# A completion semaphore of its own for the first value-weight load of a fused state-space and attention kernel

## The chip, the cores and the metric

The kernel runs on one core of one Trainium2 chip. The metric is the device time of one execution in microseconds (us). The profile gives the span from the first to the last instruction, which is about 1.8 us less than that time. Executions of one kernel within one group of runs differ by up to about 4 us (993.85 to 997.71 us in the widest case of the kernel before), and that scatter matters at the end of this text.

## The reference, cut to what matters

The reference mixes a diagonal complex state-space layer (A) and a 32-head softmax attention (B) over the same input x of 2048 rows and 1024 columns, with a gate for each row.

```python
x = A_x
g = _sigmoid((x * gate_w).sum(-1, keepdims=True))
a = _A_ref(x, A_Lambda_re, A_Lambda_im, A_B_re, A_B_im, A_C_re, A_C_im, A_log_dt, A_Dskip)
b = _B_ref(x, B_wqkv, B_wo)
return g * a + (1 - g) * b

# in _B_ref
scores = jnp.einsum("bhqd,bhkd->bhqk", q, k) * (Dh ** -0.5)
p = _softmax(scores, axis=-1)
o = jnp.einsum("bhqk,bhkd->bhqd", p, v)
```

The softmax takes 32 x 2048 x 2048 exponentials. The kernel does them on ScalarE in 1024 instructions of 128 partitions x 1024 columns.

## The kernel before

A recorder notes every operation in one order, with the tiles that it reads and writes, and works out the semaphore waits. Each DMA signals one of 14 completion semaphores, called lanes. DMAs take the lanes in turn, in the order in which they are recorded, whichever engine issues them. A DMA depends on the previous user of its lane, because the recorder counts completions by lane.

```python
# Sched.op
if dma:
    j = self.dma_rr
    self.dma_rr = (j + 1) % self.n_dma_lanes
    o.lane = "dma%d" % j
    prev = self.dma_lane_last[j]
    if prev is not None:
        d.append(prev)              # wait for the previous load on this lane
    self.dma_lane_last[j] = o
```

The order of recording at the start is this. Everything up to `opening()` is recorded before the first value-weight load, which is inside `opening()`.

```python
# build (begin() first: 2 weight loads, 9 pieces of x, 5 parameter rows: lanes in turn)
self.begin()
self.ld_b(0, 0)                    # two B tiles, real and imaginary, by SyncE
self.ld_b(1, 1)
for part in (1, 2, 0):
    self.ld_w(1, part)             # projection weights of the next head group
for j in range(8):
    self.ld_c(j)                   # 8 C tiles, real and imaginary: 16 transposes by SyncE
self.opening()
```

The opening works through a list of words. K stands for a key projection of 256 rows, B for a burst of scores with its two exponentials (a pair), Va and Vb for value projections, M for the parameters, P for a product of exponentials and values.

```python
OPENING = ("K0 B0 K1 M B1 K2 Va0 B2 Vb0 K3 Va1 B3 Vb1 Q1 Va2 K4 ..."   # cut
...
if op == "K":
    if i == 0:
        ...                        # first key and query projections
        evac(self.Q[:, 0, 0:256], 6, ("Q", 0), True, self.act)
        self.dma(lambda e: e.dma_start(self.wv0[:, :, 0:128], self.wsrc[:, :, 2048:2176]),
                 [], ["wv0"], "ld_w", "act")    # the load in question, in ScalarE's queue
```

Va0 is called "the first value product" below. The load stands in ScalarE's queue ahead of the first exponential. Va0, which reads it, stands in TensorE's queue ahead of the scores of burst B2. In the profile the load is the DMA into `f_OT` from `in_B_wqkv_dram`, as `wv0` lies in that tile.

## Time and profile before

| | before |
|---|---|
| time, median of 3 | 996.18 us (995.86 to 997.41) |
| ScalarE busy | 943.4 us (95%) |
| 1006 of the 1024 exponentials, the group written to `f_pt` | 922.8 us busy, 0.917 us each (busy time by count) |
| longest wait of ScalarE | 28.5 us, from 9.56 to 38.08 us |

The page's first rows show the stretch. Each digit is the busy share of one of 40 slices (24.9 us each) in tenths; PEclk is the granted TensorE clock in tenths.

```profile
PE   3399999999999999999999999999999999989996
ACT  0389999999999999999999999999999999999997
PEclk8599999999999999999999999999999999999998
DMA  9924203331113301321004401033201212223312
```

From the fourth slice on ScalarE is busy without a break. In the first two, TensorE is busy for about a third of the time and ScalarE for less, while the DMA engines are busy.

The exponentials are one group of the page (busy us, mean ns of one, idle time before them and what ended most of it). The mean of 1288 ns is longer than 0.917 us because the records of neighbours overlap; two in a row take 1.94 us.

```profile
L1527 ACT ACTIVATE f_pt<-f_ps 128x1024 bf16<-128x1024 f32 x1006 | 922.8, 1288 | 30.9 <-DMA f_cT_re<-in_A_C_re_dram 28.5
```

The chain of waits, as shares of the span by engine, and the waits of ScalarE (who waited for what: us in total, times, longest):

```profile
ACT 93%; SPq 3%; PE 2%; DMA 1%; DVE 1%; issue 0%; DVEq 0%
```

```profile
ACT f_pt L1527 <- DMA f_cT_re<-in_A_C_re_dram: 28.5, 1, 28.5
...
```

An exponential waits 28.5 us for a C tile, and it reads no C tile. The timeline (start in us, duration in us, engine, line, operation; idle time before it and its releaser in brackets) shows what lies between:

```profile
9.18 0.38 ACT L1125 ACTIVATE f_Q<-f_ps 128x256 bf16<-128x256 f32 x1 [3.29 <-PE f_ps L1100]
37.63 0.40 ACTq L1135 DMA_DIRECT2D f_OT<-in_B_wqkv_dram  x1
38.08 1.94 ACT L1527 ACTIVATE f_pt<-f_ps 128x1024 bf16<-128x1024 f32 x2 [28.51 <-DMA f_cT_re<-in_A_C_re_dram]
...
44.35 1.94 ACT L1527 ACTIVATE f_pt<-f_ps 128x1024 bf16<-128x1024 f32 x2 [2.41 <-PE f_ps L1521]
...
74.57 911.43 ACT L1527 ACTIVATE f_pt<-f_ps 128x1024 bf16<-128x1024 f32 x994
```

The wait belongs to the value-weight load, but its record is only 0.40 us long. The Trainium skill, "Perfetto Trace Analysis", section DMA Instruction — HWDGE (DVE, Sync), says that the profiler reports a DMA instruction from the moment when its semaphores are satisfied. This trace agrees: the record starts at 37.63 us and the wait shows only as idle time of the exponential behind it. So a DMA that blocks a queue is found by the idle time of its successor.

The last line of that timeline shows why the wait counts: 994 exponentials run from 74.57 us without a gap. Whatever ScalarE loses before, nothing makes up for.

The chain of waits in order of time (start in us, us, what) gives the rest of the story:

```profile
33.85 3.77 DMA f_cT_re<-in_A_C_re_dram
...
37.63 5.02 DMA f_OT<-in_B_wqkv_dram
...
42.70 1.05 PE f_ps L1148 x8
```

The C tile is issued at 33.85 us and lands 3.77 us later. Only then is the value-weight load issued, and it takes 5.02 us. TensorE's first value product (L1148) starts as soon as it has landed. Before the C tile, the chain is SyncE's queue from 0.91 us on, one transpose after the other, with three weight loads among them.

Last, the table by stretches of time (busy us and number of instructions of each engine, then the granted TensorE clock, the share of the DMA engines and GB/s):

```profile
14.00:38.00 24.00, 0.00 (x0) 0.00 (x0) 0.00 (x0) 0.00 (x0) 0.55 (x2) 0.53 1.15 203
```

From 14 to 38 us no matmul and no exponential runs, the clock falls to a mean of 0.53, and the DMA engines move 203 GB/s.

### The profile page before, as it was taken

How to read it: one execution, taken by the hardware profiler on the slowest of the kernel's cores; microseconds unless marked ns; L12 is line 12 of the kernel's file. 1: busy time of each engine (PE TensorE's matmuls, PEld its weight loads, DVE VectorE, ACT ScalarE, POOL GpSimd, SP SyncE). 2: the span in 40 equal slices, each digit the busy share in tenths (PEclk: the TensorE clock that was granted, in tenths of full speed). 3: DMA queues.
4: the chain of work that ended last, by engine and by line, in shares of the span. 5: the costliest groups of instructions: out<-in, count | busy, mean ns of one | idle time of the engine just before them, and what ended most of it. 6: DMA issues, size and time to landing. Idle time of an engine off the chain costs nothing.

```text
span 994.6 us, 33339 instructions
## 1 busy us (share of the span) xinstructions
PE 930.4 (94%) x15308; PEld 486.0 (49%) x15308; DVE 512.8 (52%) x1096; ACT 943.4 (95%) x1034; POOL 9.8 (1%) x39
## 2 busy tenths in 40 slices
PE   3399999999999999999999999999999999989996
PEld 1264464446444455444644554444554546444443
DVE  0178888788988823821238821158838111232223
ACT  0389999999999999999999999999999999999997
POOL 1000000000000000000000000000000000000000
PEclk8599999999999999999999999999999999999998
DMA  9924203331113301321004401033201212223312
GB/s 199 196 54 82 46 8 53 68 79 29 39 36 73 79 5 29 60 71 47 8 8 67 82 28 36 26 63 78 50 7 39 68 49 91 68 73 112 112 59 70
DMA packets 157074, 60.88 MB, mean 61 GB/s; under 512 B 145664, under 2 KB 145664, under 8 KB 156928
## 3 DMA queue, kind: packets, MB, share of 16 engines
q1 hardware_dynamic: 153728, 57.89, 26.0%
q8 instruction: 121, 1.98, 0.8%
q10 hardware_dynamic: 3200, 0.80, 0.4%
q14 instruction: 25, 0.20, 0.1%
HBM read 16.79 MB, written 12.58 MB: 30 GB/s over the span
## 4 chain that ended last, share of the span: by engine, by line
ACT 93%; SPq 3%; PE 2%; DMA 1%; DVE 1%; issue 0%; DVEq 0%
ACT f_pt L1527 92%; SPq L1032 2%; PE f_ps L1148 1%; ACT f_OT L1527 1%; SPq L1042 1%; PE f_ps L1111 1%; DMA f_OT<-in_B_wqkv_dram 1%; SPq L1048 0%; DMA f_cT_re<-in_A_C_re_dram 0%; SPq L1037 0%; DVE f_V L1153 0%; ACT f_Et L1527 0%; PE f_ps L1521 0%; DVE f_xT L1790 0%; DVE f_xT L1477 0%
## 5 line engine op out<-in xcount | busy, mean ns | idle before, releaser
L1527 ACT ACTIVATE f_pt<-f_ps 128x1024 bf16<-128x1024 f32 x1006 | 922.8, 1288 | 30.9 <-DMA f_cT_re<-in_A_C_re_dram 28.5
L1543 PEld LDWEIGHTS f_ps<-f_V,f_pt 128*128 128x128 bf16 x8048 | 234.2, 96 | 105.9 <-issue 105.6
L1543 PE MATMUL f_ps<-f_V,f_pt 128*128 128x33 bf16 x8048 | 285.4, 178 | 0.0
L1521 PE MATMUL f_ps<-f_Q,f_K 32*128 32x256 bf16 x4096 | 204.0, 274 | 52.3 <-ACT f_pt L1527 34.3
L1521 PEld LDWEIGHTS f_ps<-f_Q,f_K 32*128 32x128 bf16 x4096 | 60.6, 92 | 273.1 <-ACT f_pt L1527 240.5
L1409 PE MATMUL f_ps<-f_xT,f_wb 128*128 128x512 bf16 x512 | 131.0, 377 | 0.6
L1379 PE MATMUL f_ps<-f_xT,f_wb 128*128 128x512 bf16 x472 | 121.2, 378 | 0.1
L1328 DVE TENSOR_TENSOR_SCAN f_ht<-f_pf,f_init,f_ut 128x512 bf16<-128x512 f32 x64 | 81.0, 1275 | 0.0
L1453 DVE TENSOR_SCALAR f_Ag<-f_ps,f_gcol 128x512 f32<-128x512 f32 x32 | 24.0, 751 | 97.5 <-PE f_ps L1438 97.5
L1438 PE MATMUL f_ps<-f_cT_re,f_hp 128*128 128x512 bf16 x192 | 72.8, 379 | 0.3
L1438 PE MATMUL f_ps<-f_cT_im,f_hp 128*128 128x512 bf16 x192 | 72.6, 378 | 0.0
L1471 PE MATMUL f_ps<-f_wb,f_OT 128*128 128x512 bf16 x252 | 66.0, 381 | 0.0
L1556 DVE RECIPROCAL f_rc<-f_ps 128x8 f32<-128x8 f32 x63 | 13.1, 208 | 91.3 <-PE f_ps L1543 91.1
L1477 DVE SCALAR_TENSOR_TENSOR f_xT<-f_ps,f_gcol,f_hp 128x512 bf16<-128x512 f32 (+1 forms) x28 | 21.0, 751 | 75.3 <-PE f_ps L1471 75.3
L1397 PE MATMUL f_ps<-f_wb,f_xT 128*128 128x128 bf16 x896 | 59.2, 219 | 0.0
L1409 PEld LDWEIGHTS f_ps<-f_xT,f_wb 128*128 128x128 bf16 x512 | 40.5, 96 | 32.1 <-issue 0.7
L1415 DVE CAST f_ub<-f_ps 128x512 bf16<-128x512 f32 x48 | 33.2, 692 | 34.0 <-PE f_ps L1409 34.0
L1379 PEld LDWEIGHTS f_ps<-f_xT,f_wb 128*128 128x128 bf16 x472 | 36.8, 96 | 28.3
L1397 PEld LDWEIGHTS f_ps<-f_wb,f_xT 128*128 128x128 bf16 x896 | 50.4, 97 | 0.2
L1386 DVE CAST f_Q<-f_ps 128x512 bf16<-128x512 f32 x31 | 21.5, 692 | 49.2 <-PE f_ps L1379 49.0
L1319 DVE TENSOR_TENSOR f_tq<-f_ht,f_Et 128x512 bf16<-128x512 bf16 x128 | 46.1, 416 | 0.0
L1319 DVE TENSOR_TENSOR f_ut<-f_tq 128x512 f32<-128x512 bf16 x64 | 42.2, 684 | 0.0
(124 smaller groups left out, 493.0 us busy)
## 6 DMA issues: line engine op xcount, KB each, us to landing
ag_scratch<-f_Ag SPq DMA_DIRECT2D x32, 256.0 KB, 2.2
f_hp<-ag_scratch SPq DMA_DIRECT2D x32, 256.0 KB, 2.8
f_wb<-in_B_wqkv_dram SPq DMA_DIRECT2D x21, 256.0 KB, 4.2
out_dram<-f_xT SPq DMA_DIRECT2D x16, 256.0 KB, 2.1
f_wb<-in_B_wo_dram SPq DMA_DIRECT2D x1, 1024.0 KB, 6.5
f_OT<-f_On SPq DMA_TRANSPOSE x63, 2.3
f_wb<-in_B_wo_dram SPq DMA_DIRECT2D x1, 768.0 KB
f_wb<-in_B_wqkv_dram ACTq DMA_DIRECT2D x2, 256.0 KB, 4.3
```

The source lines that it names most:

```text
L1319: ops.append((c, lambda: dve(lambda e: e.tensor_tensor(o, a, b, op), r, w)))
L1328: ops.append((1.29, lambda ri=ri: dve(lambda e: e.tensor_tensor_scan(ht[:, ri, :], rr, ut[:, ri, :], self.init[:, ri, j:j + 1], ALU.mult, ...
L1379: mms.append((1, lambda e, f, l, a=a: e.matmul(ps[:, bank, :], w[:, g % 2, part, a, :], xT[:, a, 512 * ch:512 * (ch + 1)], start=f, stop=l ...
L1397: m = e.matmul(ps[:, bank, 128 * q:128 * (q + 1)], xT[:, a, 128 * kt:128 * (kt + 1)], w[:, g % 2, 2, a, :], start=(a == 0), stop=(a == 7))
L1409: mms.append((1, lambda e, f, l, a=a: e.matmul(ps[:, 7, :], bT[:, n % 2, ri, a, :], xT[:, a, 512 * ch:512 * (ch + 1)], start=f, stop=l), [ ...
L1415: self.dve(lambda e: e.tensor_copy(self.ub[k][:, ri, :], ps[:, 7, :]), [("bank", 7)], [("ub", k, ri)] + over, "evac_u")
L1438: mms.append((1, lambda e, f, l, j=j, ri=ri: e.matmul(ps[:, 7, :], hp[:, ri, j, cols], cT[ri][:, j, 512 * cb:512 * (cb + 1)], start=f, sto ...
L1453: self.dve(lambda e: e.tensor_scalar(a, ps[:, 7, :], self.gcol[:, 0, tt:tt + 1], None, ALU.mult), [("bank", 7), "g0"], [at], "evac_c")
L1471: mms.append((1, lambda e, f, l, j=j: e.matmul(ps[:, 7, :], OT[:, j, 256 * qb + 128 * r:256 * qb + 128 * (r + 1)], wo[j][0][:, 512 * cb:51 ...
L1521: m = e.matmul(ps[:, 2 * sl[h // 2] + h % 2, 256 * kl:256 * (kl + 1)], K[32 * h:32 * h + 32, g % 2, 128 * kt:128 * (kt + 1)], Q[32 * h:32 ...
L1527: self.act(lambda e, s=s, p=p: e.activation(self.tile[p], ps[:, 2 * s:2 * s + 2, :], ACT.Exp, scale=SCALE), [("S", s)], [("pt", p)], "exp")
L1543: m = e.matmul(ps[:, 6, o:o + 33], self.tile[p][:, h2, 256 * kl + 128 * qt:256 * kl + 128 * (qt + 1)], V[:, g % 2, 2 * i + kl, h, :], star ...
```

## The change

Its intent is to free the first value-weight load from the load that used its lane before. It adds a 15th semaphore that only this load uses; the other loads still take 14 in turn. Two signatures that pass the new argument on are cut.

```diff
-    def __init__(self, n_dma_lanes=12, pool_in_order=False, serial_xpose=False):
+    def __init__(self, n_dma_lanes=12, pool_in_order=False, serial_xpose=False, own=0):
+        self.n_rr = n_dma_lanes - own
...
         if dma:
-            j = self.dma_rr
-            self.dma_rr = (j + 1) % self.n_dma_lanes
+            j = lane
+            if j is None:
+                j = self.dma_rr
+                self.dma_rr = (j + 1) % self.n_rr
...
-  self.dma(lambda e: e.dma_start(self.wv0[:, :, 0:128], ...), [], ["wv0"], "ld_w", "act")
+  self.dma(lambda e: e.dma_start(self.wv0[:, :, 0:128], ...), [], ["wv0"], "ld_w", "act", 14)
...
-        S = Sched(n_dma_lanes=14)
+        S = Sched(n_dma_lanes=15, own=1)
```

The order of instructions is the same on every engine. The loads recorded after this one move down by one lane.

More of the change, by code (lines that the diff above doesn't have):

```diff
@@ L60, in lanes, with op @@
         return list(ENGINES) + ["dma%d" % i for i in range(self.n_dma_lanes)]
-    def op(self, eng, fn, reads=(), writes=(), deps=(), name="", dma=False, acc=(), xpose=False):
+    def op(self, eng, fn, reads=(), writes=(), deps=(), name="", dma=False, acc=(), xpose=False, lane=None):
         o = Op(eng, fn, name, dma)
@@ L1023, in pool, with dma @@
         return self.S.op("pool", fn, reads=r, writes=w, name=name)
-    def dma(self, fn, r, w, name="", eng="sp"):
-        return self.S.op(eng, fn, reads=r, writes=w, name=name, dma=True)
+    def dma(self, fn, r, w, name="", eng="sp", lane=None):
+        return self.S.op(eng, fn, reads=r, writes=w, name=name, dma=True, lane=lane)
     def ld_x(self, i, eng="sp"):
@@ L1134, in opening @@
                     evac(self.Q[:, 0, 0:256], 6, ("Q", 0), True, self.act)
-                    self.dma(lambda e: e.dma_start(self.wv0[:, :, 0:128], self.wsrc[:, :, 2048:2176]), [], ["wv0"], "ld_w", "act")
+                    self.dma(lambda e: e.dma_start(self.wv0[:, :, 0:128], self.wsrc[:, :, 2048:2176]), [], ["wv0"], "ld_w", "act", 14)
                 else:
```

## The prediction

> **What bounds the kernel now.** ScalarE's exponentials. The chain of waits gives 92% of the span to them, and the groups show 1006 of 128x1024 with 922.8 us busy, 0.917 us each; from 63.7 us to 983 us the chain is ScalarE without a break. TensorE is 94% busy but waits for ScalarE in that stage. So an idle stretch of ScalarE in the opening is paid in full. There is one: the waits of ScalarE show 28.5 us (9.56 to 38.08 us) ended by the DMA of a C tile.
>
> **Cause.** ScalarE issues the first value-weight load ("wv0") at 37.63 us, just before its first exponential. The instruction order with its waits shows that this load waits on a DMA lane. Loads take 14 lanes in turn in recording order; 39 loads (the B and C transposes too) are recorded first, so wv0 gets lane 11 behind the third C transpose, which SyncE issues at 33.85 us and which lands 3.77 us later. ScalarE's queue is in order, so the exponentials behind the load, whose scores were ready at 10.1 us, wait too. TensorE then idles until 38.9 us, and the windows show its clock fall to 0.50.
>
> **What the change does.** wv0 gets a 15th semaphore, never used before, and loses its wait. Loads recorded after wv0 move down one lane; the instruction order is equal on all engines.
>
> **Cost, step by step.**
> - wv0 issues at about 9.6 us (0.40 us of issue time), the first exponential starts near 10.1 us.
> - The DMA engines are busy from 0 to 54 us (about 200 GB/s, windows). wv0 took 5.02 us to land among C transposes; among x transposes I estimate 5 to 7: 14.6 to 16.6 us. The Trainium skill, "DMA: Bandwidth & Descriptors", section Queues, rings and completion order, says that each DMA engine takes turns between queue rows, so SyncE's backlog need not drain first; the 5.02 us, with that backlog, agree.
> - The first value product moves from 42.70 us to that landing; the third pair of exponentials from 44.35 to about 16.3 us: 28 us less.
> - x pieces must not bind: issue 7.1 to 20.0 us, landing 5.5 us later (median), so the last lands near 26 us plus 1.3 us for wv0's 256 KB; its K projection would run at about 30 us.
> - In the opening before, the matmuls of 39 to 46 us ran on the halved clock (K projection 1.89 and 1.60 us instead of 1.03). With an idle gap of 2 to 3 us only, most of that, about 0.5 to 1 us, is gained as well.
> - SyncE's queue is not moved and ends its C transposes at about 54 us; the first two output transposes (68 and 79 us before) then wait a little behind them, off the chain: their buffers and the next B tiles are needed 5 us or more later.
>
> All of it lies on the critical path, as ScalarE has no slack after.
>
> **Prediction: 967.5 us**, 8 in 10 between 965.5 and 971.5. Faster by over 2%: 0.96, within 2%: 0.03, slower: 0.01.
>
> **Signs.** ScalarE's 28.5 us wait gone, replaced by about 2 to 4 us before the third pair; wv0 issued at 9.6 us; exponentials unbroken from about 35 us; same 0.917 us each; granted clock near 1.0 in the opening; tail unchanged.
>
> **What would make it wrong.** wv0 landing late behind x transposes; x pieces landing later and stalling K projections; TensorE still cold; late output or B transposes stalling TensorE near 55 to 70 us.

## The result, and the profile after

| | before | after |
|---|---|---|
| time, median of 4 | 996.02 us (995.75 to 997.41) | 967.25 us (967.16 to 967.44) |
| ratio | 1 | 0.9709 (0.9692 to 0.9725) |
| span of the profiled execution | 994.6 us | 965.7 us |
| ScalarE busy | 943.4 us | 943.4 us |

A ratio here is the mean time of one kernel's runs over that of the other's in the same rounds, so it is not quite the ratio of the medians. The interval is a 95% interval. Executions over 1.5% slower than the fastest of the same kernel are left out of the means.

The page's first rows after the change:

```profile
PE   8999999999999999999999999999999999989995
ACT  4999999999999999999999999999999999999997
PEclk9999999999999999999999999999999999999998
```

The idle second slice is gone. ScalarE works the same 943.4 us in a span that is 28.9 us shorter. (TensorE's busy sum of 904.4 us is not comparable with 930.4 us before, as 223 matmul records are missing from this trace.)

The same group of exponentials, the chain's shares by engine, and the waits of ScalarE:

```profile
L1531 ACT ACTIVATE f_pt<-f_ps 128x1024 bf16<-128x1024 f32 x1006 | 922.8, 1288 | 2.4 <-PE f_ps L1525 2.4
```

```profile
ACT 95%; PE 3%; DVE 1%; DMA 1%; issue 0%; DVEq 0%
```

```profile
ACT L1069 <- issue: 4.5, 1, 4.5
ACT f_OT L1531 <- PE f_ps L1525: 4.4, 3, 2.5
ACT f_Q L1129 <- PE f_ps L1104: 2.9, 1, 2.9
ACT f_pt L1531 <- PE f_ps L1525: 2.4, 2, 1.8
```

SyncE's queue has left the chain, and the 28.5 us are gone. A wait of 1.8 us remains before the third pair. The timeline of ScalarE (its lines are numbered 4 higher than before):

```profile
8.83 0.38 ACT L1129 ACTIVATE f_Q<-f_ps 128x256 bf16<-128x256 f32 x1 [2.87 <-PE f_ps L1104]
8.83 0.40 ACTq L1139 DMA_DIRECT2D f_OT<-in_B_wqkv_dram  x1
9.80 1.94 ACT L1531 ACTIVATE f_pt<-f_ps 128x1024 bf16<-128x1024 f32 x2 [0.59 <-PE f_ps L1525]
...
15.49 1.94 ACT L1531 ACTIVATE f_pt<-f_ps 128x1024 bf16<-128x1024 f32 x2 [1.82 <-PE f_ps L1525]
...
45.73 911.41 ACT L1531 ACTIVATE f_pt<-f_ps 128x1024 bf16<-128x1024 f32 x994
```

The load is issued at 8.83 instead of 37.63 us, and the first exponential starts at 9.80 instead of 38.08 us. In the chain the load takes 5.00 us and is followed by the value product:

```profile
8.83 5.00 DMA f_OT<-in_B_wqkv_dram
13.84 0.05 issue
13.88 1.01 PE f_ps L1152 x8
```

The gain is made by then and is carried to the end unchanged. It is worked out here from the two traces:

| event | before | after | difference |
|---|---|---|---|
| first value product | 42.70 | 13.88 | 28.82 |
| third pair of exponentials | 44.35 | 15.49 | 28.86 |
| the 994 exponentials in a row | 74.57 | 45.73 | 28.84 |
| end of the span | 994.6 | 965.7 | 28.9 |

One thing did not come as forecast. In the table by stretches the clock of the profiled execution was again low for a while:

```profile
14.00:18.00 4.00, 4.00 (x38) 3.02 (x37) 1.37 (x7) 1.94 (x2) 0.21 (x1) 0.58 1.23 198
```

### The profile page after: what moved, and what is told of

It reads as the page before. It is cut to its first block, busy times and chain, and to the rows that moved or that the text cites. A ratio compares the mean times of both kernels' runs of the same rounds, so it can differ in the third digit from the quotient of the medians.

```text
span 965.7 us, 33117 instructions
## 1 busy us (share of the span) xinstructions
PE 904.4 (94%) x15085; PEld 486.2 (50%) x15308; DVE 512.9 (53%) x1096; ACT 943.4 (98%) x1034; POOL 9.8 (1%) x39
## 3 DMA queue, kind: packets, MB, share of 16 engines
q8 instruction: 121, 1.98, 0.9%
## 4 chain that ended last, share of the span: by engine, by line
ACT 95%; PE 3%; DVE 1%; DMA 1%; issue 0%; DVEq 0%
ACT f_pt L1531 95%; PE f_ps L1152 1%; ACT f_OT L1531 1%; PE f_ps L1086 1%; PE f_ps L1115 1%; DMA f_OT<-in_B_wqkv_dram 1%; PE f_ps L1104 0%; DVE f_V L1157 0%; ACT f_Et L1531 0%; PE f_ps L1525 0%; DVE f_xT L1794 0%; DVE f_xT L1481 0%; DVE f_ut L1749 0%; PE f_ps L1547 0%; ACT f_OT L1772 0%
## 5 line engine op out<-in xcount | busy, mean ns | idle before, releaser
L1531 ACT ACTIVATE f_pt<-f_ps 128x1024 bf16<-128x1024 f32 x1006 | 922.8, 1288 | 2.4 <-PE f_ps L1525 2.4
L1413 PE MATMUL f_ps<-f_xT,f_wb 128*128 128x512 bf16 x448 | 117.2, 377 | 9.6 <-DVE f_Ag L1457 1.5
L1383 PE MATMUL f_ps<-f_xT,f_wb 128*128 128x512 bf16 x412 | 108.2, 377 | 5.1 <-issue 0.7
L1475 PE MATMUL f_ps<-f_wb,f_OT 128*128 128x512 bf16 x218 | 57.9, 379 | 3.2
L1442 PE MATMUL f_ps<-f_cT_re,f_hp 128*128 128x512 bf16 x144 | 54.4, 378 | 0.0
```

Source lines behind the costliest of these rows:

```text
L1383: mms.append((1, lambda e, f, l, a=a: e.matmul(ps[:, bank, :], w[:, g % 2, part, a, :], xT[:, a, 512 * ch:512 * (ch + 1)], start=f, stop=l ...
L1413: mms.append((1, lambda e, f, l, a=a: e.matmul(ps[:, 7, :], bT[:, n % 2, ri, a, :], xT[:, a, 512 * ch:512 * (ch + 1)], start=f, stop=l), [ ...
L1442: mms.append((1, lambda e, f, l, j=j, ri=ri: e.matmul(ps[:, 7, :], hp[:, ri, j, cols], cT[ri][:, j, 512 * cb:512 * (cb + 1)], start=f, sto ...
L1475: mms.append((1, lambda e, f, l, j=j: e.matmul(ps[:, 7, :], OT[:, j, 256 * qb + 128 * r:256 * qb + 128 * (r + 1)], wo[j][0][:, 512 * cb:51 ...
L1531: self.act(lambda e, s=s, p=p: e.activation(self.tile[p], ps[:, 2 * s:2 * s + 2, :], ACT.Exp, scale=SCALE), [("S", s)], [("pt", p)], "exp")
```

## The experiments

Theory A: the time follows the landing of whatever load used the value-weight load's semaphore before. Rival B: any added semaphore relaxes the queues. Rival C: the gain comes from the later loads, which moved down one lane. All kernels gave a correct result. The runs were made in three groups, each on another chip with the kernel before beside it; across groups the ratios are compared, and times only roughly. In the diffs "wv0 load" stands for the whole line shown above, without its lane.

### Back on lane 11

```diff
-  wv0 load, lane 14;  S = Sched(n_dma_lanes=15, own=1)
+  wv0 load, lane 11;  S = Sched(n_dma_lanes=14)
```

> The value-weight load waits on lane 11 again, as before; all other loads keep the lanes that the change gave them (one lower than before), with 14 semaphores. Theory A (the gain is that load's wait alone): 996 us, ScalarE's wait of about 28.5 us is back. Rival C (the gain comes from the later loads that moved down one lane): it stays near 967 us.

Measured: 996.43 us (995.72 to 997.88), ratio to before 1.0006 (0.9990 to 1.0023). ScalarE's wait for the C tile is back:

```profile
ACT f_pt L1531 <- DMA f_cT_re<-in_A_C_re_dram: 28.2, 1, 28.2
```

The moved lanes of the later loads bring no gain, so rival C falls.

### Twenty lanes in turn

```diff
-  wv0 load, lane 14;      S = Sched(n_dma_lanes=15, own=1)
+  wv0 load, next in turn; S = Sched(n_dma_lanes=20)
```

> No lane of its own, but 20 lanes in turn instead of 14. The value-weight load is the 40th recorded, so it now shares lane 19 with the second imaginary B transpose, which SyncE issues at 26.0 us and which should land about 4 us later, at 30 us. Theory A (the time follows the landing of whatever load used the semaphore before): the load issues near 30 us instead of 37.6, the time is about 996.0 - 7.6 = 988.5 us, with ScalarE waiting about 20.5 us. Rival B (any added semaphores relax the queues and bring the gain): about 967 us.

Measured: 988.23 us (987.22 to 990.30), ratio 0.9925 (0.9909 to 0.9942). The timeline names the load that was waited for, and it is the B transpose:

```profile
28.75 0.40 ACTq L1139 DMA_DIRECT2D f_OT<-in_B_wqkv_dram  x1
29.19 1.94 ACT L1531 ACTIVATE f_pt<-f_ps 128x1024 bf16<-128x1024 f32 x2 [20.21 <-DMA f_wb<-in_A_B_im_dram]
```

Six added semaphores bring little more than a quarter of what one dedicated semaphore brings. Rival B falls.

### Lane 10

```diff
-  wv0 load, lane 14;  S = Sched(n_dma_lanes=15, own=1)
+  wv0 load, lane 10;  S = Sched(n_dma_lanes=14)
```

> 14 lanes, the value-weight load put on lane 10, whose previous user is the last C transpose (issued near 53 us, landing near 57 us). Theory A: the load issues near 57 us, lands 2 to 4 us later as the DMA engines are then free, and the time rises by 16 to 19 us against before, to 1012 to 1015 us. Rivals B and C: no different from the run with lane 11.

Measured, in a single run of unknown state: 1012.92 us. The load was issued at 55.21 us, behind the last C transpose, and landed 3.0 us later:

```profile
55.65 1.94 ACT L1531 ACTIVATE f_pt<-f_ps 128x1024 bf16<-128x1024 f32 x2 [46.33 <-DMA f_cT_im<-in_A_C_im_dram]
```

The times of issue and the times of the kernel now lie close to one line. From 8.83 to 55.21 us the load moves by 46.38 us, and the time by 1012.92 - 967.25 = 45.67 us. The issue at 28.75 us with 988.23 us and that at 37.63 us with 996.02 us lie within 1.4 us of it. (The times of issue are those of the profiled executions.)

### No semaphore added, only another order of recording

```diff
-  wv0 load, lane 14;  S = Sched(n_dma_lanes=15, own=1)
+  wv0 load, next in turn; S = Sched(n_dma_lanes=14)
+  ld_b, ld_w and ld_c recorded here, behind the wv0 load
...
-  ld_b, ld_w and ld_c recorded ahead of opening()
```

> 14 lanes, none reserved; instead the B, W and C loads are recorded after the value-weight load (SyncE's queue keeps its order). The load is then the 17th and shares lane 2 with the second x piece, which has landed by 8 us. Theory A: 967.2 us, the same as the changed kernel within 0.1%, with no added semaphore. Rival B (the 15th semaphore is what matters): 996 us.

Measured: 967.11 us (966.44 to 967.59), ratio 0.9709 (0.9693 to 0.9725), the same ratio as the change. The load was issued at 9.17 us. The 15th semaphore is one way to get the gain. What counts is that the load does not share a semaphore with a load that is issued late.

### Which of the two delays costs: the blocked queue or the late data?

The wait does two things: ScalarE's queue stands still, and the values come late. Two runs separate them. In the first, SyncE issues the load about as late as before, and ScalarE is free.

```diff
-  wv0 load in ScalarE's queue, lane 14
...
         for j in range(8):
             self.ld_c(j)
+            if j == 1:
+                wv0 load in SyncE's queue, lane 14
```

> The value-weight load leaves ScalarE's queue and is issued by SyncE on its own lane behind the second pair of C transposes, so that it lands about as late as before (issue about 36.5 us, landing 41 to 42.5 us; before 42.65). ScalarE is free of the wait: its first exponentials run at 10 us. Theory D (the late data are what costs, as the first value product stands in TensorE's queue before the third pair's scores): no gain but the shift of the landing, 994.5 to 996 us. Rival E (the blocked ScalarE queue is what costs): near 970 us.

In the second, the load is early, and a load of 2 KB that nothing needs blocks ScalarE's queue behind it.

```diff
   wv0 load, lane 14
+  self.dma(lambda e: e.dma_start(self.On[0:8, 1, 0, :], <A_Lambda_re as 8 rows>),
+           [], [("On", 1)], "dummy", "act", 11)
```

> The value-weight load keeps its own lane and is early (issue 8.8 us, landing 13.8 us), but a 2 KB load that nothing needs stands behind it in ScalarE's queue and waits on lane 11, so ScalarE is blocked until about 37.6 us as before. If the blocked queue alone costs (rival E), 996 us. If only the late data cost (theory D), 967 us. My expectation is that either is enough to cost nearly all: the exponentials start at 38 us as before and only the 2.4 us gap before the third pair goes, so 993 to 994 us.

Measured: the free ScalarE with late values took 994.18 us (993.69 to 995.53), ratio 0.9984 (0.9965 to 1.0003). The blocked ScalarE with early values took 996.27 us (994.48 to 997.34), ratio 0.9997 (0.9976 to 1.0017). The two timelines, the free one first:

```profile
9.72 1.94 ACT L1530 ACTIVATE f_pt<-f_ps 128x1024 bf16<-128x1024 f32 x2 [0.59 <-PE f_ps L1524]
...
42.11 1.94 ACT L1530 ACTIVATE f_pt<-f_ps 128x1024 bf16<-128x1024 f32 x2 [28.16 <-PE f_ps L1524]
```

```profile
8.83 0.40 ACTq L1139 DMA_DIRECT2D f_OT<-in_B_wqkv_dram  x1
...
38.16 1.94 ACT L1532 ACTIVATE f_pt<-f_ps 128x1024 bf16<-128x1024 f32 x2 [28.95 <-DMA f_cT_re<-in_A_C_re_dram]
...
43.23 1.94 ACT L1532 ACTIVATE f_pt<-f_ps 128x1024 bf16<-128x1024 f32 x2 [1.21 <-PE f_ps L1526]
```

With late values the first exponential starts at 9.72 us, and nothing is won. The scores of the third pair stand in TensorE's queue behind the value product, so ScalarE waits 28.16 us one step later. The 2.2 us by which the third pair is earlier than before (42.11 against 44.35) are the shift of the landing. With early values (the load landed 5.4 us after its issue at 8.83 us) and a blocked ScalarE the third pair is 1.1 us earlier (43.23 against 44.35), half of what I expected, and the timed runs show no gain. TensorE could not use the early values: its next scores waited 28.47 us for the first exponential, so that the first value product ran at 41.55 us. (In the profiled execution the 994 exponentials began 1.3 us earlier than before. They were interrupted for 0.48 us just before 891.93 us, where the clock was 0.60 from 888 to 892 us, and the wait in the tail was longer too; that wait is taken up below.) Each delay alone is enough to cost nearly all of the 28.8 us. So neither D nor E is right by itself. The change wins because it removes both.

### What is left of the opening: the clock and the remaining wait

After the change ScalarE still waits 1.82 us for the third pair. Two runs tried to take this away. One fills TensorE's idle time (12.63 to 13.88 us) with matmuls on zeros, the other records the load earlier.

```diff
                     self.pieces256(1, i, 7)
+                if i == 2:
+                    <6 matmuls 128x128 by 512 on zeros into PSUM bank 6>
```

> The changed kernel with 6 extra matmuls of 512 columns on zeros (into a PSUM bank that is free then, result overwritten) between the third K projection and the first value product, where TensorE idles 1.25 us (12.63 to 13.88 us). If that idling makes the clock fall to 0.58 in 14 to 18 us, it stays at 1.0, the matmuls of 13.9 to 17.8 us take about 2.5 us instead of 3.9, and the time falls by about 1.4 us, to 965.8 us. If the clock falls for another reason (the sparse stretch before 12.6 us), no change: 967.2 us.

```diff
   <five parameter loads in begin()>
+  wv0 load, lane 14
...
-  wv0 load, lane 14        (in opening)
```

> The changed kernel with the value-weight load recorded earlier, behind the five parameter loads (issue near 4.4 us instead of 8.8). It lands near 9.5 us, before the first value product can use it (12.7 us). If only its landing bounds the opening, the 1.8 us wait of ScalarE before the third pair shrinks to about 0.5 us: 965.8 us. Against it: 256 KB at 200 GB/s delay the second and third x pieces by up to 1.3 us, which would give the gain back: 967 us.

Measured: with filling 968.02 us (967.93 to 969.92), ratio to before 0.9723 (0.9707 to 0.9739); early 967.54 us (966.58 to 970.48), ratio 0.9720 (0.9701 to 0.9740). Neither beats the change. Their profiles nevertheless show the opening shorter: the exponentials written to `f_pt` without long gaps begin at 44.59 and 43.80 us, against 45.73 us. They are interrupted later. TensorE's waits, in the filled kernel and then in the early one:

```profile
PE f_ps L1422 <- DMA f_wb<-in_A_B_re_dram: 1.6, 1, 1.6
```

```profile
PE f_ps L1413 <- DMA f_wb<-in_A_B_re_dram: 0.7, 1, 0.7
```

TensorE waits for a B tile of the state-space part. In SyncE's queue these B tiles stand behind the 16 C transposes. Those are issued during the opening, although the first C tile is read near 188 us (217 us before). The next group of runs therefore moved the C transposes behind the 5th and 6th output transposes, and ran the change itself beside them as a control.

```diff
-        for j in range(8):
-            self.ld_c(j)
...
+        if U in (4, 5):            # behind an output transpose
+            for j in range(4 * U - 16, 4 * U - 12):
+                self.ld_c(j)
```

> The changed kernel itself, as control beside the three others on this chip: 967.2 us, within 0.2%.

> The changed kernel with the 16 C transposes taken out of the opening; SyncE issues them behind the 5th and 6th output transposes (near 99 and 113 us), well before the first fold uses them near 188 us. The changed kernel shows no wait for a late B tile, only little slack (its third B tile lands about 2 us before it is used), so on its own this should do little: 966.5 to 967.3 us; SyncE's output transpose goes out near 40 us instead of 56.8 us. If C transposes slow the opening through the DMA engines, more.

> Early value weights and late C transposes together. In the run with early value weights alone ScalarE was 1.9 us ahead of the changed kernel at 44 us and lost it again; TensorE then waited 0.7 us for a B transpose that stood behind the C transposes in SyncE's queue. Theory F (the gain of the opening is given back by late B tiles behind the C transposes): no TensorE wait for a B tile, and 1 to 1.9 us less than the changed kernel, 965.3 to 966.2 us. Rival G (given back elsewhere, by phases of lower clock): 967 us as without the move.

> The run with 6 filling matmuls, with the C transposes late. There the profile showed ScalarE 1.1 us ahead at 45 us and TensorE waiting 1.6 us for a B transpose at 73 us. Theory F: that wait is gone, 966.1 us. Rival G: 967 to 968 us as without the move.

| kernel, five runs each | median us | lowest to highest | ratio to before |
|---|---|---|---|
| the change, control | 968.62 | 966.76 to 969.69 | 0.9719 (0.9703 to 0.9735) |
| C late | 967.74 | 966.25 to 969.09 | 0.9717 (0.9703 to 0.9731) |
| C late, load early | 966.77 | 965.98 to 967.93 | 0.9707 (0.9693 to 0.9721) |
| C late, filling | 968.30 | 967.19 to 969.43 | 0.9719 (0.9705 to 0.9733) |

The control is instructive. In its profiled execution the clock of 14 to 18 us was 1.00, with no filling matmul, where the first profile of the same kernel had 0.58:

```profile
14.00:18.00 4.00, 3.55 (x54) 2.75 (x55) 1.56 (x7) 2.15 (x3) 0.31 (x1) 1.00 1.31 216
```

Its exponentials began at 44.73 us, 1.0 us earlier than in the first profile. Most of the gain was then lost to B tiles, in TensorE's waits and in ScalarE's timeline:

```profile
PE f_ps L1413 <- DMA f_wb<-in_A_B_re_dram: 2.4, 2, 1.3
```

```profile
44.73 22.25 ACT L1531 ACTIVATE f_pt<-f_ps 128x1024 bf16<-128x1024 f32 x24
67.45 7.44 ACT L1531 ACTIVATE f_pt<-f_ps 128x1024 bf16<-128x1024 f32 x8 [0.47 <-PE f_ps L1525]
75.70 881.94 ACT L1531 ACTIVATE f_pt<-f_ps 128x1024 bf16<-128x1024 f32 x962 [0.81 <-PE f_ps L1525]
```

With the C transposes late, none of the three profiles shows a wait for a B tile, and the exponentials run in one piece. This is the run with the early load:

```profile
43.83 911.43 ACT L1531 ACTIVATE f_pt<-f_ps 128x1024 bf16<-128x1024 f32 x994
```

It follows that early C transposes can hold up B tiles and that moving them removes this wait. It does not follow that the time falls by a certain amount. With filling and late C transposes the wait was gone, but the time was 968.30 us, as rival G had it and not theory F. The early load with late C transposes has the lowest median, 1.85 us under the control, but that is above the 965.3 to 966.2 us that theory F asked for, and the intervals overlap. I call that version perhaps better by one to two us, not shown to be so. Filling the idle time has no shown effect on the clock either: of four profiled executions without it and with the load issued near 9 us (the change, the control, the other order of recording, C late), only the first fell below 1.00 in 14 to 18 us.

Rival G (lower clock elsewhere takes part of the gain) is borne out by the traces. In the run with the early load alone, the B tile cost ScalarE only one gap of 0.31 us at 66.37 us. Two more gaps, 0.21 and 0.43 us, came at 860.51 and 862.88 us, where the clock was 0.72 (858 to 864 us), and the tail wait (the one wait of over a microsecond that ScalarE has after these exponentials) was 2.46 us instead of 1.77 us. The control too waited 2.45 us in the tail. In both, four matmuls just before it took 0.59 to 0.63 us each, against 0.38 us in the first profile. Over all fourteen profiles the tail wait goes with the granted clock of the stretch before it (from 3 us before the end of the last exponential to the end of the wait): 1.39 us at 1.00, 1.98 us at 0.70, 2.39 to 2.47 us at 0.61 to 0.64, and 1.76 to 1.77 us at 0.73 to 0.81 in the others. So differences of about one microsecond between single executions say little about a change in the opening. Why the clock differs from one execution to the next stays open.

## Why the prediction was right, point by point

- **The bound and the cause: right.** ScalarE's idle stretch was paid in full, 28.9 us of span for a wait of 28.5 us. Undoing only the lane brought 996.43 us back, and with the issue at 28.75 and 55.21 us the time moved along. (TensorE's next matmul ran at 39.25 us; the 38.9 us of the prediction is misread.)
- **"The exponentials behind the load ... wait too": right but incomplete.** It describes the blocked queue. The late value product in front of the third pair's scores costs just as much by itself, as the run with the free ScalarE showed.
- **Issue "at about 9.6 us": mis-sized.** It was 8.83 us. I took the end of the query copy; the trace shows that the load is issued together with that copy, both at 8.83 us, and does not wait for its end (0.38 us). The other 0.35 us came from the first projections, which ended earlier (9.18 against 8.83 us). That part is scatter and so luck: over the profiles whose ScalarE queue is the same up to this copy, it started between 8.60 and 9.27 us.
- **Landing in "5 to 7" us: right, at the low end.** It took 5.00 us among the x transposes and 5.02 us among the C transposes. The Trainium skill, "DMA: Bandwidth & Descriptors", section Queues, rings and completion order, says that each DMA engine takes turns between the queue rows. The equal 5 us behind a loaded SyncE queue fit that. No run here measured the turns themselves, and issued from SyncE's own queue among the C transposes the load took 4.1 us, so no run tells the two queues apart. In moments the landing, 13.84 us, was earlier than the 14.6 to 16.6 us of the prediction, because of the earlier issue.
- **"28 us less" for the third pair: 28.86 us.** The rest is the earlier issue, 8.83 us against the 9.6 us of the prediction.
- **"About 0.5 to 1 us" from the clock: the size right, but not there in the profiled execution.** The clock was 0.58 in 14 to 18 us, the key projection took 1.61 us and the two value products 1.01 and 1.05 us. This term and the earlier issue had opposite errors of about the same size, which is why 967.5 us met 967.25 us so closely. That is luck. The forecast took for granted that an idle gap of 2 to 3 us leaves the clock up; in the profile after the change it was down at the end of a gap of 1.25 us. In three other executions it stayed up: in the control the opening was 1.0 us shorter and that was given back, while with the other order of recording the 994 exponentials began at 44.66 us and the span, 964.7 us, kept the 1.0 us.
- **x pieces "must not bind": right.** The opening kept its pace: from the first value product to the 994 exponentials it took 31.87 us before and 31.85 us after. The slowest x piece did land later, 7.5 us after its issue instead of 5.8 us, but from 9 us on TensorE waited for an x piece only once, for 0.21 us (a weight load at 11.58 us).
- **SyncE's queue, slack of "5 us or more" for the B tiles: mis-sized.** The queue was not quite unmoved. The last C transpose was issued at 55.39 instead of 53.07 us, the first output transpose at 56.80 us, and the third real B tile at 60.02 us; TensorE read that tile at 66.31 us. It took 3.7 us to land, so the slack was a little over 2 us. In the control it was negative, 1.08 and 1.30 us: that tile was issued at 61.21 us and took 4.8 us, and TensorE was ready for it about 1 us earlier. The wall that I named under "what would make it wrong" is the next one, and its cost is about one microsecond.
- **Same 0.917 us for each exponential, unbroken from about 35 us, tail unchanged: right.** The group is busy 922.8 us in both, the unbroken row begins at 34.88 us, and the wait in the tail is 1.77 us in both.

## What to carry to other kernels

With a recorder like this one, a semaphore that several loads share in turn ties each load to the one that used it before, even when the two have nothing to do with each other and stand in different queues. Where a compute engine issues a load between its own instructions, look at what used that semaphore last and when that load is issued; record such a load before the long prefetches, or give it a semaphore of its own. And after such a wait is gone, look at the prefetches again: what was early enough on the old schedule can be in the way on the new one.

## What the Trainium skill lacked or had wrong

- "DMA: Bandwidth & Descriptors", section Rules for kernel authors, advises one dedicated semaphore for a DMA but does not give the price of a shared one in time. Here sharing 14 semaphores cost 28.8 us, and the choice of the previous user moved the time between 967 and 1013 us.
- The same page has no figure for a plain load next to a stream of transposes on the other queue. Here 256 KB took 5.02 us before and 5.00 us after to land, with the DMA engines at about 200 GB/s, and 4.3 to 5.5 us over the twelve profiles in which ScalarE issued the load while SyncE was still issuing transposes.
- "TensorE: Matmul & The Clock Gate" ties the fall of the clock to an idle window of about 3.4 us; for one other kernel it also blames frequent short idling, but gives no figure for how much of it is enough. In the profile after the change the clock fell to 0.58 (14 to 18 us) after a stretch whose longest idle gap was 1.25 us, with TensorE busy 2.35 us of the 4 us from 10 to 14 us. Another execution of the same kernel kept 1.00 at 2.33 us of 4. For the slow matmuls at the start of a kernel the page says that their number varies from run to run; these two executions show such a variation later on.
- No page that I found states in so many words whether a DMA issued from ScalarE's queue waits for the end of the instruction ahead of it. Here it did not: both started at 8.83 us (9.16 and 9.17 us with the other order of recording), right after the wait that this kernel puts into the queue ahead of that instruction as a step of its own.
